# Blocks 3 to 8 of a gated MLP in pairs: first layer as seven products of half-size sums, weight sums streamed from DRAM

## The chip, the cores and the metric

The kernel runs on one core of one Trainium2 chip. The metric is the time of one execution in device microseconds (us). The kernel before took 1048.71 us, the median of 3 runs (1047.23 to 1051.59 us). The profile is that of one further execution.

## The reference

`q`, `k` and `v` hold 8 batches of 8 heads with 576 rows of 64 values. First comes an attention whose keys and values are averaged over groups of 8 rows, so that 576 queries meet 72 keys. Its output, 4608 tokens of 512 values, goes through a root-mean-square norm and a gated MLP. In short:

```python
k_p = k.reshape(B, H, 72, 8, D).mean(axis=3);  v_p = v.reshape(B, H, 72, 8, D).mean(axis=3)
attn = softmax(q @ k_p.T / 8)
x = (attn @ v_p) as 4608 tokens x 512
xn = x / sqrt(mean(x * x) + 1e-6) * rms_g
g = xn @ w_gate;  val = xn @ w_val                  # 512 x 1536 each
out = (g * sigmoid(g) * val) @ w_out                # 1536 x 512
```

All arrays are float32.

## The kernel before, in words

**Precision.** Each operand of a large product is split into a high part (a copy in the type float32r) and a low part (the remainder). A product is then three matmuls: high weight by high x, low weight by high x, high weight by low x. `xh`, `xl` are the parts of x, `hh`, `hl` those of the hidden layer; the tiles of `w1` and `w2` (printed as `w`) hold both parts of the weights and stay on chip.

**MLP.** The tokens go in 9 blocks of 512 (`NBLK`, `NB`). d_ff is cut into 12 slices f of 128 (`NF`), d_model into 4 chunks (`NC`). For each block and f, `mm1` (L490) makes the gate slice with 12 matmuls into one PSUM bank, ScalarE takes silu of it (`gate`, L497), another 12 matmuls make the value slice into the other bank, VectorE multiplies (`val`, L502), ScalarE copies the high part `hh` (L506), VectorE subtracts for the low part `hl` (L510), and `mm2` (L521) adds 12 matmuls of the f before into four banks `po`. So one f is 36 matmuls of 512 columns. `psg` alternates between banks 2 and 3, `po` has banks 4 to 7, the attention banks 0 and 1. After f = 11 the four `po` are copied out (L527) and stored (L528).

**Attention.** It goes by head pairs, four to a batch. SyncE (SP) issues all DMAs, in program order: k (L200), q (L208) and v (L219) of a head pair come in; `s_heads` (L282) makes the scores with 10 small matmuls for each of two heads; `s_soft` (L291 to L299) is the softmax on VectorE, ScalarE and GpSimd (POOL); `s_turn` (L304) transposes the probabilities into `sq`, and twelve small DMAs (L309) gather `sq` into `pt`; `s_av` (L343) multiplies by the pooled values, and `s_square`, `s_join`, `s_sums`, `s_rms` (L378 to L404) make the norm of a batch once its four pairs are done. k and q of later pairs share one buffer (`qk`), v, `sq` and the squares share two buffers of one tag (`st`), `prob` is one buffer.

**Order.** A first phase in an order written out by hand (`ORDER`) holds batches 0 and 1, the conversion of the weights and block 0. What follows is written in program order and put in order by the compiler's scheduler: blocks 1 to 8, and between their steps the attention of batches 2 to 7 (`later_steps`, handed out by `more()` so that a block's tokens are ready when it starts). Blocks 7 and 8 have no attention beside them. `split_x` (L462, L463) multiplies by the gain and splits the tokens of a block.

## Time and profile before

| | |
|---|---|
| median of 3 runs | 1048.71 us |
| the profiled execution's own time | 1049.04 us |
| its span | 1047.3 us |
| mean granted TensorE clock | 0.980 |
| DMA, mean over the span | 62 GB/s |

The span is the time from the first to the last instruction of the core; 1.7 us of the execution lie around it. PE is TensorE's matmul, PEld its weight load, DVE is VectorE, ACT is ScalarE, POOL is GpSimd, SPq is SyncE's queue that issues the DMAs. A group's row gives busy time and the mean of one in ns, then the idle time just before its instructions and what ended it. A matmul's record lasts longer than its slot, because matmuls are pipelined: the slot is the distance between starts.

### The profile page before, as it was taken

The page shows a single profiled execution, that of the slowest core. Times are in us where ns is not written, and L with a number is a line of the kernel's source. Part 1 is how long each engine was busy: PE and PEld are TensorE (multiplying, and loading weights), DVE is VectorE, ACT ScalarE, POOL GpSimd, SP SyncE. Part 2 cuts the span into 40 slices and gives each one's busy share as a digit, 9 for nine tenths or more (in the row PEclk, how much of TensorE's full clock was granted, in tenths as well). Part 3 has the DMA queues.
Part 4 walks back from the last instruction along what each step waited for, and adds up shares of the span by engine and source line. Part 5 has one row for each costly group of instructions (what it writes and reads, how often), then busy time and mean ns, then how long its engine had stood idle before and what let it go on. Part 6 is the DMA issues. An engine that isn't in the chain of part 4 may idle for free.

```text
span 1047.3 us, 13134 instructions
## 1 busy us (share of the span) xinstructions
PE 1026.6 (98%) x4994; PEld 816.2 (78%) x4994; DVE 506.3 (48%) x857; ACT 416.6 (40%) x771; POOL 115.9 (11%) x108
## 2 busy tenths in 40 slices
PE   7899998999999999999999999999999999999998
PEld 6677776777877777777877787778777888888886
DVE  6799985635455446344653455445452431122112
ACT  5767664433443345333533354335342431121111
POOL 2313430111001100111001101110011000000000
PEclk8599999999999999999999999999999999999999
DMA  9445412222022201221122103210210010001001
GB/s 292 133 163 177 170 62 72 74 76 74 25 73 73 58 25 50 77 66 36 43 75 54 57 3 108 55 53 12 88 36 14 1 41 1 1 1 41 1 1 40
DMA packets 38702, 65.44 MB, mean 62 GB/s; under 512 B 6384, under 2 KB 20208, under 8 KB 37360
## 3 DMA queue, kind: packets, MB, share of 16 engines
q1 hardware_dynamic: 38640, 64.61, 20.3%
q8 instruction: 39, 0.64, 0.3%
q14 instruction: 23, 0.19, 0.1%
HBM read 47.19 MB, written 9.44 MB: 54 GB/s over the span
## 4 chain that ended last, share of the span: by engine, by line
PE 88%; DVE 5%; DMA 2%; ACT 2%; issue 1%; SPq 0%; ACTq 0%
PE psg L490 53%; PE po L521 27%; PE pss L282 4%; PE psx L343 3%; DVE wt L140 1%; DMA wx<-w 1%; DVE wt L144 1%; DMA main<-kT 1%; DVE wt L136 1%; ACT prob L260 1%; PE psr L412 1%; DVE w L162 0%; PE pst L323 0%; PE psb L436 0%; DMA q<-qT 0%
## 5 line engine op out<-in xcount | busy, mean ns | idle before, releaser
L490 PE MATMUL psg<-xh,w 128*128 128x512 f32 x1728 | 541.3, 395 | 2.9 <-ACT xh L462 2.9
L490 PEld LDWEIGHTS psg<-xh,w 128*128 128x128 f32 x1728 | 322.3, 189 | 82.9 <-ACT xraw L350 3.4
L490 PE MATMUL psg<-xl,w 128*128 128x512 f32 x864 | 338.2, 392 | 0.0
L521 PE MATMUL po<-w,hh 128*128 128x512 f32 x864 | 223.3, 395 | 0.0
L502 DVE TENSOR_TENSOR act<-act,psg 128x512 f32<-128x512 f32 x108 | 73.6, 682 | 288.1 <-PE psg L490 254.5
L521 PEld LDWEIGHTS po<-w,hh 128*128 128x128 f32 x864 | 162.6, 188 | 37.7
L490 PEld LDWEIGHTS psg<-xl,w 128*128 128x128 f32 x864 | 162.6, 188 | 35.5 <-DVE xl L463 0.7
L506 ACT CAST hh<-act 128x512 fp32r<-128x512 f32 x108 | 67.1, 622 | 212.5 <-DVE act L502 212.4
L497 ACT ACTIVATE act<-psg 128x512 f32<-128x512 f32 x108 | 64.5, 597 | 204.8 <-PE psg L490 202.6
L521 PE MATMUL po<-w,hl 128*128 128x512 f32 x432 | 122.4, 395 | 0.4 <-DVE hl L510 0.4
L521 PEld LDWEIGHTS po<-w,hl 128*128 128x128 f32 x432 | 79.5, 188 | 20.3 <-DVE act L502 2.0
L510 DVE TENSOR_TENSOR hl<-act,hh 128x512 fp32r<-128x512 f32 x102 | 70.0, 686 | 40.9 <-ACT hh L506 38.5
L299 POOL TENSOR_TENSOR prob<-prob,sm 128x360 f32<-128x360 f32 x48 | 38.7, 826 | 446.2 <-DVE sm L297 257.9
L497 ACT ACT_TABLE_LOAD x40 | 51.3, 1283 | 47.8 <-PE psg L490 26.6
L291 DVE TENSOR_REDUCE mx<-pss 128x5 f32<-128x360 f32 x48 | 23.4, 528 | 49.8 <-PE pss L282 49.6
L304 DVE STREAM_TRANSPOSE sq<-prob 128x960 f32<-128x960 f32 x24 | 28.3, 1179 | 38.8 <-POOL prob L299 34.6
L384 POOL TENSOR_TENSOR acc<-acc,sq 128x576 f32<-128x576 f32 x21 | 30.7, 1461 | 146.4 <-ACT sq L378 146.4
L239 DVE TENSOR_REDUCE pv<-v 72x128 f32<-72x1024 f32 x28 | 34.0, 1214 | 22.8 <-PE psx L343 21.5
L282 PEld LDWEIGHTS pss<-pk,q 64*128 64x128 f32 x560 | 34.5, 193 | 12.0 <-issue 8.9
L282 PE MATMUL pss<-pk,q 64*128 64x72 f32 x560 | 38.6, 283 | 1.8 <-DVE own L329 0.9
L294 ACT ACTIVATE prob<-prob 128x360 f32<-128x360 f32 x48 | 23.1, 505 | 31.9 <-DVE prob L293 31.8
L343 PE MATMUL psx<-pt,pv 72*64 72x256 f32 (+2 forms) x224 | 35.4, 429 | 0.0
(90 smaller groups left out, 701.2 us busy)
## 6 DMA issues: line engine op xcount, KB each, us to landing
wx<-w SPq DMA_DIRECT2D x10, 1024.0 KB
v<-vN SPq DMA_DIRECT2D x32, 288.0 KB
out<-o SPq DMA_DIRECT2D x36, 256.0 KB
wx<-w SPq DMA_DIRECT2D x16, 512.0 KB
k<-kT SPq DMA_DIRECT2D x28, 288.0 KB
q<-qT SPq DMA_DIRECT2D x28, 288.0 KB
pt<-sq SPq DMA_DIRECT2D x96, 40.0 KB
pt<-sq SPq DMA_DIRECT2D x96, 32.0 KB
```

The source lines that it names most:

```text
L239: nc.vector.tensor_reduce(pv, s["v"], AX.X, ALU.add)
L282: nc.tensor.matmul(s["ps", h][:, t * SP:(t + 1) * SP], s["q"][r, o:o + P], s["pk"][r, :], start=True, stop=True)
L299: nc.gpsimd.tensor_tensor(pr, pr, sm[:, :, None].broadcast_to(shape), ALU.mult)
L304: nc.vector.transpose(sq.rearrange("p b g j -> p g b j"), prob.rearrange("p g (b j) -> p g b j", b=3))
L343: nc.tensor.matmul(ps[r, :n], s["pv"][:, r], s["pt"][:, h, tok], start=True, stop=True)
L384: nc.gpsimd.tensor_add(acc[b], acc[b], st[b, p]["sq"])
L490: nc.tensor.matmul(ps[:, :NB], w[:, c, cols], x[c], start=(j == 0), stop=(j == len(todo) - 1))
L497: nc.scalar.activation(t, ps[:, :NB], AF.Silu)
L502: nc.vector.tensor_mul(t, t, ps[:, :NB])
L506: nc.scalar.copy(a, st["act"])
L510: eng.tensor_sub(l, st["act"], hh[i, f].bitcast(F32))
L521: nc.tensor.matmul(po[i][t], x[i, f][:, t * P:(t + 1) * P], w, start=(f == 0 and k == 0), stop=(f == NF - 1 and k == 2))
```

## The change

**Blocks 1 and 2** are computed as before, with two additions. The attention is handed out faster: three batches (2 to 4) are finished here, where before it was one for each block; the other three batches are spread over the pairs (3,4) and (5,6). And `w_parts` makes, for each f, the seven weight operands of a seven-product scheme and writes them to DRAM: three are blocks of the first-layer weights and are copied by DMA (L532, eight a slice), four are sums and differences, made on POOL (L537 to L542), split by ScalarE (L546) and POOL (L547) and written (L548). The sums use the tag `st`, the split ones the tag `out`, of two buffers each.

**Blocks 3 to 8** go in pairs (3,4), (5,6), (7,8). For one f the pair's tokens (two blocks), the two halves of d_model and the two kinds of columns (gate, value) make a 2x2 by 2x2 block product. In place of eight block products of 6 matmuls, seven are made (`PRODUCTS`, in Winograd's form), so 42 matmuls in place of 48. The operands of x (`XP`: three blocks, four sums) are made once for a pair by `halves`; the weight operand of each product, 256 KB, comes from DRAM through a ring of 8 slots (`next_part`, L608), and the next load is written behind each product. The results are combined on VectorE (L828, L837, L841, L845, L851, L852, L855) and ScalarE (a copy L825, silu L834 and L842); the products alternate between bank 2 (`px`, `pv`) and bank 3 (`py`, `pz`, `pw`). The first block's `mm2` is run in two halves inside the next f; its hidden layer is split at L658 (`hh`) and L662 (`hl`, one buffer as before). The second block's hidden layer is kept in `hb`, and its twelve `mm2` run after the pair's twelve f, with `halves` of the next pair written between them.

**Smaller edits.** The norm's last step multiplies by the gain as well: four operations of 288 elements (L419) for each half in place of one of 4x288 (L404). `ones` is one column that is broadcast. `keep_tail` keeps the end of a batch that the next pair needs.

What the order shows. SyncE's queue in block 1, before: between the loads of one head pair and its gathering copies stands nothing else (`k`, `v`, `q`, `pt` as above).

```order
L219 DMA v_3_1914<-vN 72x1024
L200 DMA k_3_1912<-kT 128x576
L208 DMA q_3_1933<-qT 128x576
L309 DMA pt_2_1937<-sq_2_1935 32x2x128 x2
L309 DMA pt_2_1937<-sq_2_1935 32x2x160 x2
```

The same place in the changed kernel; `parts` are the weight operands in DRAM, `wt` the split sums.

```order
L214 DMA k_3_1898<-kT 128x576
L532 DMA parts_2349<-w_4_772 128x2x128 x4
L548 DMA parts_1807<-wt_1_1914 128x512
L233 DMA v_3_1900<-vN 72x1024
L548 DMA parts_1807<-wt_2_1918 128x512
L222 DMA q_3_1928<-qT 128x576
L532 DMA parts_2349<-w_4_772 128x2x128
L532 DMA parts_2579<-w_5_906 128x2x128
L548 DMA parts_1807<-wt_3_1922 128x512
L548 DMA parts_1807<-wt_4_2004 128x512
L532 DMA parts_2579<-w_5_906 128x2x128
L323 DMA pt_2_1932<-sq_2_1930 32x2x128 x2
```

Two of the four writes of a slice now stand ahead of the q load and two ahead of the gathering copies of the pair; each waits for POOL and ScalarE to make its tile.

TensorE in block 1 before, f = 9 with the `mm2` of f = 8 behind it (the end of the value slice, `psg_9_1`):

```order
L490 MATMUL psg_9_1_3189<-xh_2_2460,w_9_1213 128x512 x2
L490 MATMUL psg_9_1_3189<-xl_2_2464,w_9_1213 128x512
L490 MATMUL psg_9_1_3189<-xh_3_2461,w_9_1213 128x512 x2
L490 MATMUL psg_9_1_3189<-xl_3_2465,w_9_1213 128x512
L521 MATMUL po_0_2637<-w_8_1138,hl_8_3155 128x512
L521 MATMUL po_1_2638<-w_8_1138,hl_8_3155 128x512
L521 MATMUL po_2_2639<-w_8_1138,hl_8_3155 128x512
L521 MATMUL po_3_2640<-w_8_1138,hl_8_3155 128x512
L521 MATMUL po_0_2637<-w_8_1138,hh_8_3153 128x512 x2
```

TensorE in the last pair of the changed kernel: the last product of f = 2 (`pw_2`, weight operand `wp_2_6`), then f = 3 (`xp` are the operands of x).

```order
L614 MATMUL pw_2_7732<-xp_S_7347,wp_2_6_7651 128x512 x6
L614 MATMUL px_3_7763<-xp_A_7283,wp_3_0_7666 128x512 x6
L614 MATMUL py_3_7773<-xp_S_7326,wp_3_1_7682 128x512 x6
L614 MATMUL px_3_7763<-xp_A_7368,wp_3_2_7692 128x512 x3
L673 MATMUL po_0_7603<-w_2_604,hl_2_7760 128x512
L673 MATMUL po_1_7604<-w_2_604,hl_2_7760 128x512
L673 MATMUL po_0_7603<-w_2_604,hh_2_7758 128x512 x2
L673 MATMUL po_1_7604<-w_2_604,hh_2_7758 128x512 x2
L614 MATMUL px_3_7763<-xp_A_7368,wp_3_2_7692 128x512 x3
L614 MATMUL pz_3_7799<-xp_S_7389,wp_3_3_7707 128x512 x6
```

Before, 24 matmuls of L490 stand between the value slice of an f and the first `mm2` that reads its `hl`; now 15 matmuls stand between the last product of an f and that `mm2`. At the end of a pair none do (f = 11, then the second block's f = 0):

```order
L614 MATMUL pw_11_8514<-xp_S_7347,wp_11_6_8445 128x512 x6
L673 MATMUL po_0_7603<-w_11_1418,hl_11_8538 128x512
L673 MATMUL po_0_7603<-w_11_1418,hh_11_8536 128x512 x2
L673 MATMUL po_1_7604<-w_11_1418,hl_11_8538 128x512
L673 MATMUL po_1_7604<-w_11_1418,hh_11_8536 128x512 x2
L673 MATMUL po_2_7605<-w_11_1418,hl_11_8538 128x512
```

There the `mm2` of f = 11 follows the last product directly.

VectorE at the end of pair (3,4), between the combination of f = 11 and its `hl`: `acc` and `xraw` belong to the norm of batch 6, `xp_A` to `halves` of the next pair.

```order
L419 SCALAR_TENSOR_TENSOR xraw_4844<-xraw_4844,gcol,acc_4854 128x288 x4
L837 TENSOR_TENSOR u_4227<-u_4227,pz_11_5636 128x512
L416 RECIPROCAL acc_4854<-acc_4854 128x288
L841 TENSOR_TENSOR hb_8_5242<-u_4227,pv_11_5646 128x512
L419 SCALAR_TENSOR_TENSOR xraw_4844<-xraw_4844,gcol,acc_4854 128x288
L845 TENSOR_TENSOR u_4227<-u_4227,pw_11_5657 128x512
L419 SCALAR_TENSOR_TENSOR xraw_4844<-xraw_4844,gcol,acc_4854 128x288 x3
L855 TENSOR_TENSOR hb_8_5242<-hb_8_5242,u_4227 128x512
L851 TENSOR_TENSOR u_4227<-u_4227,pw_11_5657 128x512
L577 TENSOR_TENSOR xp_A_5826<-u_4227,xp_A_5826 128x2x320
L852 TENSOR_TENSOR act_11_5634<-act_11_5634,u_4227 128x512
```

The norm of a batch now stands among the combining operations; before, `L404` stood beside `L502` and `L510` alone.

The diff, cut to its core:

```diff
+FIRST = 3
+PRODUCTS = (("A11", "B11"), ("S2", "T2"), ("A12", "B21"), ("S3", "T3"), ("A22", "T4"), ("S1", "T1"), ("S4", "B22"))
+RING = [f"x{j}{c}" for c in range(NC) for j in "hl"]
...
-        x = xraw[b][:, :, tok]
-        nc.vector.tensor_mul(x, x, r[:, None, :].broadcast_to([P, NC, n]))
+        for c in range(NC):
+            x = xraw[b][:, c, tok]
+            nc.vector.scalar_tensor_tensor(x, x, gcol[:, c:c + 1], r, ALU.mult, ALU.mult)
...
+    def w_parts(f, k):
...
+        if k is None:
+            for name in PARTS:
+                if name in BLOCKS:
+                    for h in (0, 1):
+                        nc.sync.dma_start(wparts[f][PARTS.index(name)][:, h], block(W1[f][:, h].bitcast(F32), name))
+            return
+        G = nc.gpsimd
+        if k == 0:
+            t = sb2.tile([P, NC, 2 * P], F32, tag="st", name=f"wsum{f}")
+            G.tensor_add(t, W1[f][:, 0].bitcast(F32), W1[f][:, 1].bitcast(F32))
+            d = WP["sum"] = sb2.tile([P, 4, 2, P], F32, tag="st", name=f"wdif{f}")
+            G.tensor_sub(d[:, 0], block(t, "B12"), block(t, "B11"))
...
+        d = WP["sum"][:, k - 1]
+        y = sb2.tile([P, 2, 2, P], F32R, tag="out", name=f"wt{f}_{k}")
+        nc.scalar.copy(y[:, 0], d)
+        G.tensor_sub(y[:, 1], d, y[:, 0].bitcast(F32))
+        nc.sync.dma_start(wparts[f][PARTS.index(f"T{k}")], y.bitcast(F32))
...
+    def halves(i, n):
...
+        nc.scalar.copy(X[:, 0], y)
+        V.tensor_sub(X[:, 1], y, X[:, 0].bitcast(F32))
...
+    def next_part():
+        n = len(ring)
+        if n < len(todo_parts):
+            i, f, k = todo_parts[n]
+            w = ring[i, f, k] = sb1.tile([P, 2, 2, P], F32R, tag=RING[n % len(RING)], name=f"wp{i}_{f}_{k}")
+            nc.sync.dma_start(w.bitcast(F32), wparts[f][k])
+
+    def product(i, f, k, ps, start, stop):
+        w, x = ring[i, f, k], XP[i, PRODUCTS[k][0]]
+        todo = [(c, h) for c in range(2) for h in ((0, 0), (1, 0), (0, 1))]
+        for j, (c, (a, b)) in enumerate(todo):
+            nc.tensor.matmul(ps[:, :NB], w[:, a, c, :], x[:, b, c, :],
+                             start=start and j == 0, stop=stop and j == len(todo) - 1, skip_group_check=not start)
+        next_part()
...
-    mm2(*pend)
+    for i in range(FIRST, NBLK, 2):
+        j = i + 1
...
+            x = bank(2, f"px{i}_{f}")
+            product(i, f, 0, x, True, True)
+            nc.scalar.copy(h, x)
+            y = bank(3, f"py{i}_{f}")
+            product(i, f, 1, y, True, True)
+            nc.vector.tensor_add(u2, h, y)
+            more()
+            if pend:
+                mm2(*pend, (0, 1))
+            product(i, f, 2, x, False, True)
+            t = st["act"] = sb1.tile([P, NB], F32, tag="act", name=f"act{i}_{f}")
+            nc.scalar.activation(t, x, AF.Silu)
+            y = bank(3, f"pz{i}_{f}")
+            product(i, f, 3, y, True, True)
+            nc.vector.tensor_add(u3, u2, y)
+            more()
+            x = bank(2, f"pv{i}_{f}")
+            product(i, f, 4, x, True, True)
+            nc.vector.tensor_sub(h, u3, x)
+            nc.scalar.activation(h, h, AF.Silu)
+            y = bank(3, f"pw{i}_{f}")
+            product(i, f, 5, y, True, True)
+            nc.vector.tensor_add(u3, u3, y)
+            more()
+            if pend:
+                mm2(*pend, (2, 3))
+            pend = (i, f)
+            product(i, f, 6, y, False, True)
+            nc.vector.tensor_add(u2, u2, y)
+            nc.vector.tensor_mul(t, t, u2)
+            act_hi(i, f)
+            act_lo(i, f, nc.vector)
+            nc.vector.tensor_mul(h, h, u3)
+            more()
+        mm2(*pend)
+        pend = None
+        for f in range(NF):
+            st["act"] = hb[f // 4][:, f % 4]
+            act_hi(j, f)
+            act_lo(j, f, nc.vector)
+            mm2(j, f)
+            if j + 1 < NBLK and f < len(XPARTS):
+                halves(j + 1, ORDER_X[f])
```

## The prediction

> **What bounds the kernel now.** I read the page first, for the busy shares and the chain.

> ```profile
> span 1047.3 us, 13134 instructions
> ...
> PE 1026.6 (98%) x4994; PEld 816.2 (78%) x4994; DVE 506.3 (48%) x857; ACT 416.6 (40%) x771; POOL 115.9 (11%) x108
> ...
> PE 88%; DVE 5%; DMA 2%; ACT 2%; issue 1%; SPq 0%; ACTq 0%
> PE psg L490 53%; PE po L521 27%; PE pss L282 4%; PE psx L343 3%; DVE wt L140 1%; DMA wx<-w 1%; DVE wt L144 1%; DMA main<-kT 1%; DVE wt L136 1%; ACT prob L260 1%; PE psr L412 1%; DVE w L162 0%; PE pst L323 0%; PE psb L436 0%; DMA q<-qT 0%
> ```

> TensorE is the bound: the two layers of the MLP (L490, L521) are 80% of the span in the chain that ends last. So a matmul that goes is worth a whole slot. What a slot is shows the chain in order of time, in blocks 7 and 8, where no attention runs.

> ```profile
> 843.00 5.47 PE psg L490 x24
> ...
> 1024.32 5.47 PE psg L490 x24
> ```

> From 843.00 to 1024.32 lie 22 slices f, each 24 matmuls of L490 and 12 of L521: 181.32 / 22 = 8.242 us a slice, 8.242 / 36 = 0.2289 us a matmul, without a wait. A block with attention beside it, from the table of windows (block 3):

> ```profile
> 401.60:512.40 110.80, 110.80 (x550) 87.77 (x549) 52.97 (x96) 44.93 (x69) 10.78 (x11) 1.00 0.19 54
> ```

> 110.80 less 12 x 8.242 = 98.9 leaves 11.9 us, or 2.98 us of TensorE for each of four head pairs. TensorE does not stop there either. So before has hardly a wait after the first phase, and whatever the change makes TensorE wait is added in full.

> **What is removed.** In each pair of blocks and each f, 42 matmuls replace 48: 3 x 12 x 6 = 216 slots of 0.2289 = 49.4 us less. Moved attention (four head pairs of 2.98 us into blocks 1 and 2) sums to nothing on TensorE.

> **What is added, one: the chain of a pair's f.** The operations of the hidden layer and the hand-over from TensorE:

> ```profile
> L502 DVE TENSOR_TENSOR act<-act,psg 128x512 f32<-128x512 f32 x108 | 73.6, 682 | 288.1 <-PE psg L490 254.5 <-issue 33.6
> L510 DVE TENSOR_TENSOR hl<-act,hh 128x512 fp32r<-128x512 f32 x102 | 70.0, 686 | 40.9 <-ACT hh L506 38.5 <-PE po L521 2.4
> L506 ACT CAST hh<-act 128x512 fp32r<-128x512 f32 x108 | 67.1, 622 | 212.5 <-DVE act L502 212.4
> L497 ACT ACT_TABLE_LOAD x40 | 51.3, 1283 | 47.8 <-PE psg L490 26.6 <-DVE hl L510 21.0
> ...
> 334.23 0.39 PE L490 MATMUL psg<-xl,w 128*128 128x512 f32 x1
> 334.72 0.69 DVE L502 TENSOR_TENSOR act<-act,psg 128x512 f32<-128x512 f32 x1 [6.50 <-PE psg L490]
> 335.44 0.62 ACT L506 CAST hh<-act 128x512 fp32r<-128x512 f32 x1 [2.90 <-DVE act L502]
> ```

> The last matmul's slot ends at 334.23 + 0.23 = 334.46 and VectorE starts at 334.72, 0.26 later; ScalarE follows VectorE after 0.03. In the pair, `hl` of an f comes after the last product through u2, act, `hh` and `hl`: 0.26 + 0.69 + 0.69 + 0.03 + 0.62 + 0.05 + 0.69 = 3.0 us, and its `mm2` stands 15 slots behind, 15 x 0.2289 = 3.4 us. The cover is 0.4 us, where before 24 slots (5.5 us) less 2.3 left 3.2. The banks have as little: a bank is refilled 6 slots (1.37 us) after its product, and one VectorE operation takes 0.26 + 0.69 = 0.95 of it, 0.4 to spare; a table load of 1.28 us ahead of silu does not fit. The VectorE work is eight operations of 0.69 in 12.4 us, so it is place in the queue, not load, that can stall. Where the next f's u2 (L828, which waits 12 slots, 2.75) is ahead of `hl` in VectorE's order, `hl` is there after 2.75 + 0.26 + 0.69 + 0.69 = 4.4, about 1 us late. I take 0.17 us for each of 36 f, 6 us; 0 if all covers hold, 10 if `hl` is late by 0.3 each time.

> **Two: attention inside the pairs.** Eleven to twelve head pairs run there, each with these on VectorE, the first three twice:

> ```profile
> L293 DVE TENSOR_TENSOR prob<-pss,mx 128x360 f32<-128x360 f32 x48 | 23.7, 522 | 0.0
> L291 DVE TENSOR_REDUCE mx<-pss 128x5 f32<-128x360 f32 x48 | 23.4, 528 | 49.8 <-PE pss L282 49.6
> L296 DVE TENSOR_REDUCE sm<-prob 128x5 f32<-128x360 f32 x48 | 23.0, 521 | 0.3
> L304 DVE STREAM_TRANSPOSE sq<-prob 128x960 f32<-128x960 f32 x24 | 28.3, 1179 | 38.8 <-POOL prob L299 34.6 <-DMA pt<-sq 4.2
> L228 DVE TENSOR_REDUCE pk<-k 128x72 f32<-128x576 f32 x28 | 21.0, 751 | 22.9 <-DMA k<-kT 22.9
> L239 DVE TENSOR_REDUCE pv<-v 72x128 f32<-72x1024 f32 x28 | 34.0, 1214 | 22.8 <-PE psx L343 21.5 <-DMA v<-vN 1.1
> L402 DVE RECIPROCAL acc<-acc 128x288 f32<-128x288 f32 x12 | 23.4, 1952 | 13.1 <-ACT acc L401 13.0
> L463 DVE SCALAR_TENSOR_TENSOR xl<-xraw,gcol,xh 128x320 fp32r<-128x320 f32 x8 | 4.3, 543 | 2.3 <-ACT xh L462 2.3
> ```

> 2 x (0.522 + 0.528 + 0.521) + 1.179 + 0.751 + 1.214 = 6.3 us a head pair. VectorE takes them in order among the combining operations, whose banks have 0.4 us to spare: each of the three long ones that comes at a wrong time costs up to 0.8. Before, a bank had 12 slots, so they cost nothing. I take 0.85 us for 11 head pairs, 9.5, and 2.5 for the norms of three batches: 12, between 5 (one collision in two head pairs) and 25 (three in each).

> **Three: the seams.** After the last product of a pair nothing is left for TensorE but the `mm2` that waits for `hl`: the chain of 3.0 and a weight load of about 0.2, 3.2 us, at three seams. `hl` has one buffer, so the second block's first `hl` waits until the `mm2` of f = 11 has read it, 1 us more: 4.2 each, 12.6. At the end of pair (3,4) the norm of batch 6 stands in VectorE's queue ahead of `hl`: two reciprocals of 1.95 and eight scaled copies of some 0.5 (the 0.543 of 128x320 bounds one) are 8 us, of which I take 6.4 as uncovered. At both inner seams `halves` puts seven steps into the second block's f.

> ```profile
> L162 DVE TENSOR_TENSOR w<-wt,w 128x1024 fp32r<-128x1024 f32 x6 | 7.3, 1215 | 0.0
> ```

> Four sums at 2 x 1.215 and three splits at 1.215 are 13.4 us, with twelve `hl` 21.7, against 12 x 12 slots of TensorE, 33 us: hidden but for the start, 1.8. Together 12.6 + 6.4 + 1.8 = 20.8, taken as 21, between 14 and 28.

> **Four: the clock at the seams.** The one long wait of before outside the first phase shows what follows one (timeline and windows):

> ```profile
> 178.61 0.73 PE L490 MATMUL psg<-xh,w 128*128 128x512 f32 x2 [2.91 <-ACT xh L462]
> 186.52 1.34 PE L282 MATMUL pss<-pk,q 64*128 64x72 f32 x20 [0.18 <-DMA q<-qT]
> ...
> 178.00:181.00 3.00, 2.39 (x7) 1.55 (x8) 2.69 (x8) 2.96 (x8) 0.00 (x0) 0.85 0.97 295
> 181.00:184.00 3.00, 3.00 (x9) 2.34 (x9) 1.90 (x4) 0.48 (x1) 0.00 (x0) 0.58 0.76 205
> ```

> After 2.91 us without work the granted clock fell to 0.58, and 24 matmuls took 186.34 - 178.61 = 7.73 in place of 5.47, 2.3 us more. All three seams wait 3.2 or more, but the last has little left behind it: 2 x 2.3, taken as 4, between 0 and 7. [...]

> **Five: the first pair's start.** Its ring loads and the last of its operands come behind gathering copies and a dense VectorE queue: 4, between 0 and 8 (one burst of copies, below).

> **Six: blocks 1 and 2.** SyncE issues in order. A burst of gathering copies and what follows it:

> ```profile
> 195.54 8.21 SPq L309 DMA_DIRECT2D pt<-sq  x12
> 203.85 0.38 SPq L200 DMA_DIRECT2D k<-kT  x1
> 205.12 1.18 DVE L304 STREAM_TRANSPOSE sq<-prob 128x960 f32<-128x960 f32 x1 [4.15 <-DMA pt<-sq]
> ...
> L162 POOL TENSOR_TENSOR w<-wt,w 128x1024 fp32r<-128x1024 f32 x4 | 10.0, 2503 | 21.4 <-ACT w L158 21.4
> L299 POOL TENSOR_TENSOR prob<-prob,sm 128x360 f32<-128x360 f32 x48 | 38.7, 826 | 446.2 <-DVE sm L297 257.9 <-DVE sm L298 188.3
> ```

> The burst issues for 8.2 us and lands 205.12 - 203.75 = 1.4 later. `wdif` shares the two buffers of `sq`, so POOL begins it only then. POOL takes 2.5 us for 1024 elements; one of 256 lies between 2.5 / 4 = 0.63 and the 0.83 of 360, and I take 0.75. Four differences are 3.0, two low parts 1.5, their writes' landing 1.4 (the `out` tag has two buffers), the other two low parts 1.5, their writes' issue 0.8; then the next burst. A round is 17.8 us. Three batches and one head pair ahead are 13 rounds, 231, and with the first softmax (186.52 to 195.54, 9.0) and a last step of about 10, 250. TensorE has 24 x 8.242 + 12 x 2.98 = 233.6. The difference is 17 (a prolonged wait at `psx` for `pt`, since TensorE too is in order); 2 if rounds overlap, 40 if the four writes are each late by a landing.

> **The sum.** 6 + 12 + 21 + 4 + 4 + 17 = 64 us of waits against 49.4: 1049.0 + 14.6 = 1063.6, so 1064. The profiled execution is 0.3 above the median of the runs, which is within the spread; the span lies 1.7 below it.

> **The rivals.**

> *The queues stay ahead* (faster). Every wait above supposes that an operation stands where I put it in its queue. If a round in blocks 1 and 2 takes under 233.6 / 13 = 18.0 us with its ends overlapped, TensorE sets the pace there and term six falls to 1. VectorE at some 6.3 us more in each second f is likewise far from full, so that collisions come to 8 and the chain to 2; the seams' floor is 12.6 and the norm is covered: 14; clock 3, start 1. Waits 29, 1049.0 - 49.4 + 29 = 1029. For it: VectorE is busy 48%, ScalarE 40%. Against: 0.4 us of cover.

> *No change.* Half of term six and a cheaper seam, waits of 44 to 55: 1049 (1044 to 1054). For it stands that each term's lower half suffices.

> *The ring starves* (slower still). A ring load is issued when its slot is read, some 7 products (9.6 us) to a whole f (12.4) ahead of its use. Behind a burst of 8.2 and a landing of 1.4, with up to four loads queued, it comes up to 4 us late, at each of 11 bursts: 44 more, 1108. The loads before:

> ```profile
> k<-kT SPq DMA_DIRECT2D x28, 288.0 KB
> ```

> A pair needs 7 x 256 KB in 12.36 us, 148 GB/s; in the window 178 to 181 above, loads of 288 KB moved at 295 GB/s. So bandwidth speaks against it and SyncE's order for it. [...]

> **How the numbers follow.** The forecast as reasoned (its own range 1054 to 1090) 0.44, the queues ahead 0.31, no change 0.13, the starving ring 0.12. A difference of 0.5% (5 us) is about what a measurement of this kernel can tell. So faster 0.31, same 0.13, slower 0.56. The range: all low ends together, 0 + 5 + 14 + 0 + 0 + 2 = 21 us of waits, give 1021, so it begins at 1020; at the top, terms six and two halfway to their high ends (+18) and the ring late at a third of the bursts (+14) give 1096.

> **What would show it.** In the changed profile: periods of 54 slots in pair (7,8), 12.4 us if clean, 12.7 with term one; idle time ahead of `po` reading `hl` at each seam, 3 us and more; idle ahead of `psx` in blocks 1 and 2 released by `pt`; granted clock under 1.0 after the seams. Idle time ahead of a product released by a DMA of `wp` means the ring. The forecast is wrong if blocks 1 and 2 show no such idle time, or if TensorE's idle time after block 0 sums to under 45 us.

## The result, and the profile after

The changed kernel took 1115.49 us, the median of 4 runs (1110.75 to 1116.32), against 1049.18 us for the kernel before on the same chip: a ratio of 1.062, with a 95% interval of 1.058 to 1.066. It is slower by 66 us, and not by the 15 that were forecast; the time lies above the range. The matmuls went as counted (49.4 us), so TensorE lost some 116 us to other things where 64 were expected. The page of the changed kernel:

```profile
span 1113.0 us, 14084 instructions
...
PE 1038.7 (93%) x4778; PEld 790.1 (71%) x4778; DVE 669.7 (60%) x1090; ACT 451.8 (41%) x843; POOL 221.6 (20%) x216
...
PEclk8599998999989789999999999999999999999999
...
PE 60%; DVE 16%; DMA 7%; issue 5%; SPq 4%; ACT 4%; POOL 3%; POOLq 0%; DVEq 0%; ACTq 0%
```

TensorE now has 60% of the chain that ends last, where it had 88%, and the row of the granted clock is under 9 tenths in the slices 12, 14 and 15 of the 40, which lie in blocks 1 and 2. TensorE's busy time did not fall although 216 matmuls went (1038.7 us, 1026.6 before): where the granted clock was 0.50 each took longer. In one such stretch, from 446.71 to 449.70, seven matmuls of 512 columns start 0.43 us apart, against 0.23 at a clock of 1.00. The table of windows shows the stages: first blocks 1 and 2 of the kernel before, then of the changed kernel blocks 1 and 2 and the three pairs. A stage runs from its first matmul to the first of the next; the columns are those of the first line.

```profile
core 0: us, PE busy (x) PEld busy (x) DVE busy (x) ACT busy (x) POOL busy (x), PEclk, DMA share, GB/s
178.61:401.60 222.99, 222.81 (x1107) 176.04 (x1108) 114.63 (x208) 92.34 (x144) 22.76 (x24) 0.99 0.22 61
```

```profile
181.11:491.56 310.45, 275.59 (x1296) 200.63 (x1297) 192.84 (x334) 145.54 (x247) 143.09 (x148) 0.91 0.48 142
491.56:717.86 226.30, 216.66 (x996) 162.96 (x995) 146.74 (x253) 91.14 (x137) 18.49 (x19) 0.99 0.50 151
717.86:919.00 201.14, 195.68 (x862) 151.85 (x861) 106.21 (x167) 64.64 (x98) 7.40 (x7) 1.00 0.43 127
919.00:1109.09 190.09, 186.41 (x787) 147.17 (x785) 76.74 (x113) 37.22 (x63) 0.00 (x0) 0.99 0.39 115
```

How many head pairs lie in blocks 1 and 2 is read from the scores (20 records each) and from psx (8 each):

```profile
L296 PE MATMUL pss<-pk,q 64*128 64x72 f32 x320 | 25.2, 277 | 8.9 <-DMA q<-qT 7.8 <-ACT xraw L364 0.7 <-DVE xraw L366 0.4
L357 PE MATMUL psx<-pt,pv 72*64 72x256 f32 (+1 forms) x112 | 21.6, 467 | 12.7 <-DMA pt<-sq 9.2 <-issue 3.3
```

That is 16 scores and 14 psx, on the mean 15 head pairs. The counts of matmuls in the windows also show that the last 12 of block 2's `mm2` run in pair (3,4), and that six matmuls of the next pair's first product run ahead of the border of (5,6) and of (7,8). The stages against their slots:

| stage | time | slots | lost |
|---|---|---|---|
| blocks 1 and 2 | 310.5 | 24 x 8.242 + 15 x 2.98 - 12 x 0.2289 = 239.8 | 71 |
| pair (3,4) | 226.3 | 12 x 66 x 0.2289 + 6.5 x 2.98 + 18 x 0.2289 = 204.8 | 22 |
| pair (5,6) | 201.1 | 181.3 + 2.5 x 2.98 = 188.8 | 12 |
| pair (7,8) | 190.1 | 181.3 - 6 x 0.2289 = 179.9 | 10 |

The three pairs lost 44 us together. Blocks 1 and 2, which keep the old form, lost 71. (Block 1 began 2.5 us later than before; in the traces of all runs it begins between 176.7 and 181.6.) The waits of TensorE that the profile names in the whole changed kernel, the largest first:

```profile
PE po L673 <- DVE hl L662: 13.8, 12, 3.2
PE psx L357 <- DMA pt<-sq: 9.2, 6, 3.9
PE pss L296 <- DMA q<-qT: 7.8, 8, 1.5
...
PE px L614 <- DMA wp<-parts: 0.9, 1, 0.9
```

Before, the hand-over from hl cost 0.4 us in all, the q loads 0.2, and psx had no wait:

```profile
PE po L521 <- DVE hl L510: 0.4, 1, 0.4
...
PE pss L282 <- DMA q<-qT: 0.2, 1, 0.2
```

The ring hardly ever made TensorE wait (0.9 us).

**The clock in blocks 1 and 2.** One less the granted clock, summed over blocks 1 and 2, makes 27 us there and 1.7 in the same blocks before. TensorE was at work for 47.4 of the 54.6 us at half clock (16 windows at 0.50), so by the clock's share 23.7 us of work were lost to it. TensorE was idle for 34.9 us (310.45 less 275.59). How the rest of the 71 parts was not measured. In the changed kernel's trace every change of the clock falls on a grid of 3.413 us with one phase for the whole run: 27 stretches at one clock in a row last 1 to 114 whole steps of it. Two pairs of neighbouring grid windows:

```profile
214.61:218.02 3.41, 1.95 (x24) 1.50 (x22) 2.16 (x2) 0.81 (x2) 2.39 (x3) 1.00 0.89 283
218.02:221.44 3.42, 3.42 (x12) 2.63 (x10) 1.85 (x4) 0.32 (x1) 1.37 (x1) 0.50 0.38 110
```

```profile
276.05:279.46 3.41, 1.72 (x9) 1.25 (x8) 2.38 (x2) 1.53 (x4) 1.42 (x2) 1.00 0.18 45
279.46:282.87 3.41, 3.41 (x30) 2.69 (x29) 3.41 (x3) 2.42 (x4) 3.25 (x5) 1.00 0.68 197
```

In the first window TensorE did 20 small matmuls of the scores and 4 of 512 columns, was idle 1.46 us, and the next window ran at half clock. In the second pair's first window it was idle longer, 1.69 us, but did 7 of 512 columns, and the clock held. Some 15 of 512 columns fit in a window (3.413 / 0.2289).

### The profile page after: what moved, and what is told of

It is laid out like the page before. It is cut to its first block, busy times and chain, and to the rows that moved or that the text cites. A ratio compares the mean times of both kernels' runs of the same rounds, so it can differ in the third digit from the quotient of the medians.

```text
span 1113.0 us, 14084 instructions
## 1 busy us (share of the span) xinstructions
PE 1038.7 (93%) x4778; PEld 790.1 (71%) x4778; DVE 669.7 (60%) x1090; ACT 451.8 (41%) x843; POOL 221.6 (20%) x216
## 4 chain that ended last, share of the span: by engine, by line
PE 60%; DVE 16%; DMA 7%; issue 5%; SPq 4%; ACT 4%; POOL 3%; POOLq 0%; DVEq 0%; ACTq 0%
PE po L673 20%; PE pw L614 8%; PE px L614 7%; PE psg L642 6%; PE pz L614 4%; PE pv L614 4%; PE py L614 4%; SPq L323 4%; PE pss L296 3%; PE psx L357 2%; DVE xraw L419 1%; DMA q<-qT 1%; DVE wt L154 1%; DMA k<-kT 1%; DVE acc L416 1%
## 5 line engine op out<-in xcount | busy, mean ns | idle before, releaser
L642 PE MATMUL psg<-xh,w 128*128 128x512 f32 x576 | 196.2, 421 | 3.0 <-ACT xh L507 2.9
L673 PEld LDWEIGHTS po<-w,hh 128*128 128x128 f32 x864 | 166.4, 193 | 38.8 <-issue 0.8
L642 PEld LDWEIGHTS psg<-xh,w 128*128 128x128 f32 x576 | 113.6, 201 | 37.6 <-issue 7.9
L642 PE MATMUL psg<-xl,w 128*128 128x512 f32 x288 | 119.9, 419 | 0.0
L614 PE MATMUL px<-xp_A,wp 128*128 128x512 f32 x432 | 118.5, 397 | 0.9 <-DMA wp<-parts 0.9
L614 PE MATMUL pw<-xp_S,wp 128*128 128x512 f32 x432 | 113.5, 397 | 2.0 <-DVE u L845 1.5
L614 PEld LDWEIGHTS pw<-xp_S,wp 128*128 128x128 f32 x432 | 80.4, 188 | 24.1 <-DVE u L845 3.7
L614 PEld LDWEIGHTS px<-xp_A,wp 128*128 128x128 f32 x432 | 80.5, 188 | 22.2 <-DMA wp<-parts 1.8
L837 DVE TENSOR_TENSOR u<-u,pz 128x512 f32<-128x512 f32 x36 | 24.7, 686 | 86.3 <-PE pz L614 86.2
L642 PEld LDWEIGHTS psg<-xl,w 128*128 128x128 f32 x288 | 57.5, 200 | 16.8 <-issue 3.5
L662 DVE TENSOR_TENSOR hl<-act,hh 128x512 fp32r<-128x512 f32 x66 | 49.1, 743 | 32.5 <-ACT hh L658 32.5
L825 ACT COPY hb<-px 128x512 f32<-128x512 f32 x36 | 21.1, 585 | 111.7 <-PE px L614 111.7
L658 ACT CAST hh<-act 128x512 fp32r<-128x512 f32 x72 | 44.7, 620 | 52.0 <-DVE act L852 29.5
L614 PE MATMUL pz<-xp_S,wp 128*128 128x512 f32 x216 | 57.0, 397 | 0.7 <-DVE u L828 0.7
L614 PE MATMUL pv<-xp_A,wp 128*128 128x512 f32 x216 | 56.8, 398 | 0.0
L842 ACT ACTIVATE hb<-hb 128x512 f32<-128x512 f32 x36 | 22.7, 632 | 83.4 <-DVE hb L841 83.1
## 6 DMA issues: line engine op xcount, KB each, us to landing
v<-vN SPq DMA_DIRECT2D x32, 288.0 KB
k<-kT SPq DMA_DIRECT2D x28, 288.0 KB
```

The costliest lines, as they stand in the source:

```text
L614: nc.tensor.matmul(ps[:, :NB], w[:, a, c, :], x[:, b, c, :], start=start and j == 0, stop=stop and j == len(todo) - 1, skip_group_check=no ...
L642: nc.tensor.matmul(ps[:, :NB], w[:, c, cols], x[c], start=(j == 0), stop=(j == len(todo) - 1))
L658: nc.scalar.copy(a, st["act"])
L662: eng.tensor_sub(l, st["act"], hh[i, f].bitcast(F32))
L673: nc.tensor.matmul(po[i][t], x[i, f][:, t * P:(t + 1) * P], w, start=(f == 0 and k == 0), stop=(f == NF - 1 and k == 2))
L837: nc.vector.tensor_add(u3, u2, y)
```

## The experiments

Each time is the median of two or four runs, beside runs of the kernel before on the same chip (1049 to 1051 us).

| run | us | ratio, 95% interval |
|---|---|---|
| changed kernel | 1115.5 | 1.062 (1.058 to 1.066) |
| e1 operands of one slice | 1077.5 | 1.027 (1.024 to 1.030) |
| e2 copies only | 1075.9 | 1.025 (1.022 to 1.028) |
| e3 sums only | 1118.5 | 1.066 (1.063 to 1.069) |
| e4 writes on ScalarE's queue | 1125.8 | 1.073 (1.068 to 1.078) |
| e5 no first sum | 1091.6 | 1.039 (1.035 to 1.043) |
| e6 no writes | 1112.3 | 1.058 (1.055 to 1.061) |
| e7 split bursts | 1108.7 | 1.055 (1.044 to 1.066) |
| e8 even pace | 1117.9 | 1.064 (1.061 to 1.067) |
| e9 one tile | 1104.0 | 1.052 (1.049 to 1.056) |
| e10 one tile, split bursts | 1117.6 | 1.065 (1.060 to 1.070) |
| e11 one tile, pairs from block 5 | 1093.4 | 1.041 (1.038 to 1.044) |
| e12 one slice, split bursts | 1094.6 | 1.043 (1.039 to 1.047) |
| e13 filler | 1120.2 | 1.068 (1.064 to 1.071) |
| e14 one tile, VectorE | 1096.5 | 1.046 (1.042 to 1.050) |
| e15 as e14, pairs from block 5 | 1077.7 | 1.027 (1.023 to 1.031) |
| e16 two hl | 1108.6 | 1.057 (1.054 to 1.060) |
| e17 one slice, pairs from block 5 | 1066.6 | 1.016 (1.014 to 1.018) |

### What in blocks 1 and 2: the making of the operands, or the pace

e1 makes the operands of one slice, and the ring reads that slice for all twelve; the matmuls stay the same in number, though they no longer compute this MLP:

```diff
-    todo_w = [(f, k) for f in range(NF) for k in (None, 0, 1, 2, 3, 4)]
+    todo_w = [(0, k) for k in (None, 0, 1, 2, 3, 4)]
...
-            nc.sync.dma_start(w.bitcast(F32), wparts[f][k])
+            nc.sync.dma_start(w.bitcast(F32), wparts[0][k])
```

> The weight operands are made for one slice f alone and every ring load reads that slice; eleven twelfths of the copies, sums, splits and writes are left out of blocks 1 and 2, and the attention keeps its faster pace. Blocks 1 and 2 took 313 us in the changed kernel (178.6 to 491.7), where 24 slices and some 13 head pairs are worth 236 us of TensorE. Theory A (making the operands is what holds the attention up): these blocks fall to 240 to 255 us and the time to 1040 to 1058 us. Theory B (the faster pace of the attention holds TensorE up by itself): the blocks stay at 290 or more, the time at 1090 or more.

```profile
177.40:448.97 271.57, 255.99 (x1297) 192.43 (x1297) 176.47 (x335) 132.41 (x206) 47.84 (x49) 0.96 0.30 86
```

Neither: 38 us went, and blocks 1 and 2 still took 271.6 us, 32 more than their 239.8 of slots. So the making of the operands costs 38, and about 32 are lost with hardly any of it: 15.6 of idle TensorE (271.57 less 255.99), 10 by the clock, and some 6 that no run parts. What else the change puts in these blocks is the faster attention; that it is the cause of the 32 is argued, not shown. For it speaks where the idle time stands: some 12 of the 15.6 us ahead of the attention's own matmuls.

```profile
L296 PE MATMUL pss<-pk,q 64*128 64x72 f32 x320 | 23.6, 279 | 4.8 <-DMA q<-qT 4.7
L357 PE MATMUL psx<-pt,pv 72*64 72x256 f32 (+1 forms) x112 | 18.3, 425 | 5.5 <-DMA pt<-sq 4.7 <-PE psx L357 0.7
L413 PE MATMUL psr<-sums,ones 128*128 128x288 f32 x12 | 2.8, 303 | 1.8 <-DVE sums L405 1.8
```

e2 and e3 part the making into copies and sums; the ring reads slice 0 for what is not made:

```diff
-    todo_w = [(f, k) for f in range(NF) for k in (None, 0, 1, 2, 3, 4)]
 e2:
+    todo_w = [(f, k) for f in range(NF) for k in (None, 0, 1, 2, 3, 4) if f == 0 or k is None]
 e3:
+    todo_w = [(f, k) for f in range(NF) for k in (None, 0, 1, 2, 3, 4) if f == 0 or k is not None]
```

> All copies of weight blocks to DRAM (eight a slice) are made, the sums for one slice alone. Theory A1 (POOL, the shared buffers of sq, v, wsum and wdif, and the writes that wait for them make the round long): within 12 us of the run with one slice. Theory A2 (SyncE's issue time of 96 small copies makes the round long): at least half of the loss is still there, 1080 us or more.

> All sums, splits and their writes are made, the copies of blocks for one slice alone. Theory A1: 1095 us or more, nearly the changed kernel's 1115. Theory A2: 1075 us or less.

The copies cost nothing that can be measured (1075.9 against 1077.5); the sums cost all of it (1118.5). There are 72 copies, six for a slice: three blocks in two halves each, and not eight as the text on the change has it. SyncE's time to issue them is not the price.

### What in the sums: the writes, the buffers or POOL's time

e4 moves copies and writes to ScalarE's queue (`nc.scalar.dma_start`), e6 leaves the writes of all slices but one out (`if f == 0:` ahead of L548); its ring reads slice 0 for the sums.

> All copies and writes of weight operands are issued from ScalarE's queue in place of SyncE's. If their place in SyncE's order ahead of the q load and the gathering copies is what counts, 1050 to 1085 us. If the shared buffers and POOL's order count, 1100 us or more; ScalarE then also waits at the writes, ahead of its exponentials, and it can be slower than 1115.

> All sums and splits are made, but only the first slice's are written to DRAM, so that 44 writes that wait in SyncE's queue for POOL are left out; the ring reads the first slice's sums. Theory W: 1085 us or less. Theory S: 1100 us or more. Between them, both.

Without the writes it is 3 us less (1112.3), which the two intervals don't tell from nothing, and moving copies and writes makes it 10 slower. The prediction had 2.2 us for the writes' landing and issue in every round; next to none of that is on the path.

e5 takes the differences from the high parts alone; e9 makes the same sums in the same order of rounding, but in one tile:

```diff
 e5:
-            t = sb2.tile([P, NC, 2 * P], F32, tag="st", name=f"wsum{f}")
-            G.tensor_add(t, W1[f][:, 0].bitcast(F32), W1[f][:, 1].bitcast(F32))
+            t = W1[f][:, 0].bitcast(F32)
 e9:
-            d = WP["sum"] = sb2.tile([P, 4, 2, P], F32, tag="st", name=f"wdif{f}")
-            G.tensor_sub(d[:, 0], block(t, "B12"), block(t, "B11"))
...
+            b11, b12, b21, b22 = WP["sum"] = [block(t, x) for x in ("B11", "B12", "B21", "B22")]
+            G.tensor_sub(b11, b12, b11)
+            G.tensor_sub(b12, b22, b12)
+            G.tensor_sub(b22, b22, b11)
+            G.tensor_sub(b21, b22, b21)
```

> The differences are taken from the high parts of the weights alone: the sum of 1024 elements on POOL and its tile wsum are left out, so that of the two buffers that sq, v and the squares share only one is taken by a slice. The sums cost 38 us (1115 against 1077 with one slice). Theory S (the shared buffers couple POOL's work to the bursts and the v loads): 1088 to 1102 us. Theory P (POOL's time itself): 12 x 2.5 us of POOL less and no more than a tenth of it on the path, 1108 to 1114. Theory W (the writes that wait in SyncE's queue): unchanged, 1113 to 1118.

> The same four sums with the same operations on POOL, but each difference is written over a block of wsum that is no longer needed, so that wdif is gone and a slice takes one of the two shared buffers in place of two. Theory S (the shared buffers): 1088 to 1100 us, as without the first sum (1091.6). Theory P (POOL's 2.5 us for the first sum was what that run saved): 1108 to 1117.

e5 saves 24 us and e9, which frees the buffer but keeps the sum, 11.5. If such savings add up, which no run tests, about 11.5 of the 38 are the shared buffer, 12.4 the first sum's time on POOL, at most 3 the writes, and the rest the differences and splits. Much of what is saved is clock. Blocks 1 and 2 of e9:

```profile
181.28:481.53 300.25, 269.17 (x1317) 194.92 (x1317) 196.09 (x345) 147.47 (x252) 145.20 (x150) 0.95 0.49 146
```

TensorE is idle 31.1 us where it was 34.9, but the loss to the clock is 15 where it was 27. How the buffer acts is seen in the chain of the changed kernel, in order of time:

```profile
390.89 1.17 POOL wdif L539
...
393.50 0.74 POOL wdif L542
394.25 3.55 DMA v<-vN
397.83 1.23 DVE pv L253
...
399.14 1.19 DVE sq L318
...
402.00 0.64 SPq L323
```

The v load is issued when POOL has done with the buffer of `wsum` (394.25), VectorE waits for v, and behind that wait in VectorE's order stands the transposition that the next burst of gathering copies needs: 11 us from POOL's first difference to the burst.

e14 gives the sums in one tile, and the low parts of the split ones, to VectorE (`G = nc.vector`).

> The sums in one tile, and made by VectorE in place of POOL (VectorE takes 1.2 us for 1024 elements where POOL takes 2.5). Theory P (POOL's time in the round, 12 us of the 38): 1085 to 1098. Rival (VectorE is 60% busy in blocks 1 and 2 and its queue gets the wait in POOL's place): 1104 or more.

1096.5 us: 7.5 us below e9. The runs of the two kernels do not overlap (at most 1100.5 here, at least 1101.8 there), though their intervals do a little. So POOL's speed was part of the round, though VectorE is the busier engine (60% against POOL's 20% in the changed kernel). In the changed kernel POOL took 2.49 us for the first sum, of 128x1024, and VectorE 1.22 for an operation of that size (L598); a difference, of 128x256, took POOL 0.82 and an operation of that size VectorE 0.42 (L591, L594):

```profile
L537 POOL TENSOR_TENSOR wsum<-w 128x1024 f32<-128x1024 f32 x12 | 29.8, 2486 | 5.6 <-DMA pt<-sq 3.3 <-DMA v<-vN 1.6
L539 POOL TENSOR_TENSOR wdif<-wsum 128x256 f32<-128x256 f32 x12 | 9.8, 817 | 28.2 <-DMA pt<-sq 21.0 <-DVE pv L253 5.8 <-issue 1.3
```

### The rounds: bursts, pace, and where the pairs begin

e7, e10 and e12 issue every second gathering copy from ScalarE's queue:

```diff
-                nc.sync.dma_start(
+                (nc.scalar if a % 2 else nc.sync).dma_start(
                     t[32 * i:32 * i + n, :, o:o + w],
```

> Six of the twelve gathering copies of each head pair are issued from ScalarE's queue, so that a burst takes about 4 us of SyncE's queue in place of 8. Theory B (the burst is the longest link of a round, and rounds pace blocks 1 and 2): up to 4 us less in each of 14 rounds, 1065 to 1095 us. Rival (ScalarE pays 3.6 us a burst ahead of its own work, and the round is held elsewhere): 1110 to 1130.

> One tile for the sums and six of the twelve gathering copies on ScalarE's queue. If buffers and bursts are two separate holds: about 7 us below the run with one tile alone. If the same rounds are meant: no difference, or some us more by ScalarE's issue time.

> Weight operands for one slice alone, and half of each burst on ScalarE's queue. 30 us were lost in blocks 1 and 2 without the sums. If SyncE's burst of 8 us is the long link of those rounds: 1058 to 1070 us. If not: 1073 to 1085, with ScalarE's issue time.

7 us less on the changed kernel (with an interval that takes in the changed kernel's own ratio), 14 more beside one tile, 17 more beside one slice. The waits of ScalarE in e7 show the price: its queue waits at a copy whose `sq` isn't there and then issues six copies, up to 8.2 us, and `hh` stands behind them.

```profile
ACT hh L658 <- DMA pt<-sq: 38.9, 6, 8.2
```

So whether the burst's 8 us are the long link can't be told from these runs; the other queue costs as much as it frees.

e8 delays batch 5 to block 3:

```diff
+    goals.append((single + 15, goals[-1][1]))
     for i in range(FIRST, NBLK - 2, 2):
-        goals.append((goals[-1][0] + (15 if i == FIRST else 0) + 4 * NF, ends[min(B, -(-(i + 4) * NB // S)) - 3]))
+        goals.append((goals[-1][0] + 4 * NF, ends[min(B, -(-(i + 4) * NB // S)) - 3]))
```

> Batch 5 starts with block 3 and not in the last part of block 2, so that two head pairs fewer run in blocks 1 and 2. Theory B (each round there costs TensorE some 5 us beyond its own work): blocks 1 and 2 come down by 15 to 18 us, of which 6 is moved work, and the time is 1100 to 1108. Rival (the last blocks' batches have to be ready anyway and the lost time moves to pair (3,4)): 1112 to 1119.

```profile
180.93:479.98 299.05, 269.21 (x1221) 198.36 (x1221) 178.94 (x303) 135.00 (x232) 140.31 (x143) 0.90 0.47 140
479.98:721.40 241.42, 226.51 (x1071) 169.77 (x1070) 157.30 (x283) 100.92 (x151) 23.55 (x24) 0.97 0.50 151
```

The rival holds: blocks 1 and 2 come down by 11 us, of which 2.5 head pairs of moved work are 7.5, pair (3,4) goes up by 15, and the time is the same within the noise (1117.9). A head pair moved from one crowded place to the next brings nothing.

e11, e15 and e17 begin the pairs at block 5 (`FIRST = 5`, and one buffer for the pooled k and the softmax's small tiles): with one tile on POOL, with one tile on VectorE, with the operands of one slice.

> One tile for the sums, and the pairs begin at block 5: blocks 1 to 4 as before, the sums spread over four blocks, five batches of attention in four blocks in place of three in two, 144 matmuls (33.0 us) less than before in place of 216; the pooled k and the small tiles of the softmax have one buffer, to make room. If waits come from crowding two blocks: blocks 1 to 4 lose 25 us or less, the two pairs 9 and 25: 1049 - 33 + 59 = 1075 or less. If each slice and each round costs the same wherever it is: 1085 to 1100.

> The sums in one tile on VectorE, and the pairs beginning at block 5. If the two help separately: 1093 less 6 to 18 us, 1075 to 1087. If not: 1090 or more.

> Weight operands for one slice alone (the rest left out), pairs beginning at block 5: what the pairs would be worth if their weight operands cost nothing and the attention had four blocks in place of two. 33.0 us of slots less than before; the two pairs lost 24 us beyond their slots in the runs from block 5. If the attention's pace in four blocks (some 22 head pairs, where before had 16) loses 10 us or less: 1042 to 1052. If each head pair over the old pace costs some 4 to 5 us, as in blocks 1 and 2 without sums: 1060 to 1075.

e11 fell into the second alternative, 11 us under e9; e15 gained separately, to 1077.7, the fastest here with all operands made. e17 takes the sums away from it and is still 1.6% slower than before:

```profile
177.42:664.81 487.39, 474.95 (x2364) 364.58 (x2363) 271.25 (x518) 213.51 (x335) 64.26 (x68) 0.98 0.25 72
```

48 slices and 22 head pairs, less the 12 matmuls that run in the next pair, are 395.6 + 65.6 - 2.7 = 458.5; 29 are lost with hardly any operand made, 12.4 of it idle and 8.5 by the clock. No start of the pairs that was run pays: at block 5 33.0 us of slots are saved, the two pairs lose about 25 beyond their slots, and the blocks ahead of them 29.

### The clock

e13 adds four matmuls of 512 columns ahead of the first psx of a head pair; the scheduler puts them some slots earlier:

```diff
+        if 2 <= b <= 5 and u == 0:
+            for _ in range(4):
+                nc.tensor.matmul(ps, W2[0][:, 0, :P], W2[0][:, 0, :], start=True, stop=True)
```

> Four matmuls of 512 columns whose result is overwritten stand in TensorE's order ahead of the first psx of each head pair of batches 2 to 5, 13 us of extra slots for 14 head pairs in blocks 1 and 2. There the clock fell to half in whole stretches of 3.41 us, after stretches with at most 4 matmuls of 512 columns; 27.3 us were lost to it. Theory C (a sparse stretch brings the half clock, and a wait before psx takes extra work at no cost): the loss to the clock falls to 15 us or less, TensorE's idle time by some 10, and the time is 1100 to 1115. Rival (the extra work only adds its slots, the waits move along): 1123 to 1135, with a loss to the clock as before.

Half and half. The loss to the clock fell from 27 to 15 us while 60 matmuls (13.7 us) were added, as theory C has it; but the waits moved along, as the rival has it:

```profile
177.46:492.37 314.91, 281.05 (x1368) 206.62 (x1367) 196.92 (x342) 144.68 (x248) 141.27 (x150) 0.95 0.47 139
```

TensorE is idle for 33.9 us (34.9 before the filler). So most of the work was paid for by the clock and not by the waits: the blocks took some 5 us more, and 1120 us in all is no gain.

### The seams

e16 gives hl two buffers (`sb2.tile` for `sb1.tile` in `act_lo`); to make room, the pooled k and the softmax's small tiles have one.

> hl has two buffers (the pooled k and small tiles of the softmax have one, to make room). By the prediction's third term one buffer costs 1 us at each of the three seams: 1109 to 1114 us, and the first mm2 of a second block no longer waits for hl. Rival (the chain through hh and hl sets it, not the buffer): 1114 to 1118.

1108.6: the time asked for, but not at the place. From the start of the last product to the end of TensorE's work it is 42.5 us (43.2 in the changed kernel), 0.7 less for one seam, and the first wait there stays 2.88:

```profile
1064.31 0.79 PE L673 MATMUL po<-w,hl 128*128 128x512 f32 x1 [2.88 <-DVE hl L662]
```

Blocks 1 and 2, which have the second buffer too, took 5.4 us less (305.1). So at a seam the chain sets the wait, and the buffer little.

## Why the prediction was wrong

**What is removed** was right: slots of 0.2289 us, 216 of them.

**The chain of a pair's f** was under-sized. Pair (7,8), chain in order of time:

```profile
944.29 1.48 PE po L673 x6
...
1058.27 1.48 PE po L673 x6
```

Nine periods in 113.98 us make 12.66 a slice: 0.30 beyond 12.36, where 0.17 was taken; 36 slices make 11 us and not 6. Only 0.1 of it is hl coming late. Six matmuls of a product take 1.40 us from start to start and not 1.373, seven times 0.027 a slice; why they do was not tested. The prediction looked for waits and took every slot for equal.

**The seams** had the chain right and the rest of the term too large. The last one, from the timeline:

```profile
1065.87 1.56 PE L614 MATMUL pw<-xp_S,wp 128*128 128x512 f32 x6
...
1068.91 0.62 ACT L658 CAST hh<-act 128x512 fp32r<-128x512 f32 x1 [4.28 <-DVE act L852]
...
1069.56 0.69 DVE L662 TENSOR_TENSOR hl<-act,hh 128x512 fp32r<-128x512 f32 x1 [0.68 <-ACT hh L658]
1070.31 0.50 PE L673 MATMUL po<-w,hl 128*128 128x512 f32 x1 [2.88 <-DVE hl L662]
...
1078.45 1.20 PE L673 MATMUL po<-w,hl 128*128 128x512 f32 x4 [0.38 <-DVE hl L662]
```

2.88 us of idle where 3.2 were worked out (of these 0.2 for a weight load; those of L521 took 0.19 on the mean before), and 0.38 for the one buffer where 1 was. The norm ahead of `hl` at pair (3,4)'s end cost little, though 6.4 was taken for it: TensorE was idle for 3.24 us there. The first waits at the two inner seams:

```profile
677.30 0.51 PE L673 MATMUL po<-w,hl 128*128 128x512 f32 x1 [3.24 <-DVE hl L662]
...
881.36 0.50 PE L673 MATMUL po<-w,hl 128*128 128x512 f32 x1 [1.48 <-DVE hl L662]
```

At the middle seam six matmuls of the next pair's first product fill the time ahead. All waits for `hl` at the three seams sum to 9 us, where the third term had 21. Behind the last wait 24 matmuls (5.5 us) take from 1070.31 to 1078.45, 8.1: a clock window of 3.41 us at 0.50, from 1071.35, takes 1.7 of it. After block 2 one clock window fell at pair (3,4)'s end and one here, 3.4 us in all where the fourth term had 4. The three pairs lost 44 us; terms one to five were 6 + 12 + 21 + 4 + 4 = 47. That these agree is in part luck: the first term was too small by 5 and the third too large. How attention, start and seam share the 22 of pair (3,4) was not parted by a run.

**Blocks 1 and 2** is the step that failed: 17 us, between 2 and 40, where 71 were lost. Two figures of its sum were too small, and one loss was missing. The number of rounds: "Three batches and one head pair ahead are 13 rounds", but the pace's next goal begins 15 places before block 2 ends, and 15 bursts start there. And the round, 17.8 us:

```profile
198.15 8.22 SPq L323 DMA_DIRECT2D pt<-sq  x12
...
488.77 8.10 SPq L323 DMA_DIRECT2D pt<-sq  x12
```

14 rounds in 290.6 us are 20.8. In the prediction's own sum they give 290.6 + 9 + 10 = 310 against 242.5 of slots, 67 lost. This shows how far off the term's sizes were, but it proves no cause: 20.8 is the measured time over the number of rounds, and whatever made TensorE wait is in it, the clock too. In the kernel with one slice 15 bursts start from 195.59 to 436.74, 17.2 us each. With the sums all but gone a round is thus nearly as long as was predicted with them; the sums add 3.6. What makes the round long was named only in part: the wait of wdif for sq is there, the writes are hardly (3 us or less, e6), and the way through the v load and VectorE's order was missed. The wait that was foreseen, psx for pt, is 9.2 of TensorE's 34.9 us of idle time in these blocks; 7.8 stand ahead of the scores, for q, and 8.4 ahead of psr, for the norm's sums.

**The clock** was charged at two seams and nowhere else. In blocks 1 and 2 it took 23.7 of the 71. The prediction quoted one wait of 2.91 us and the half clock after it, and read from it that long waits bring it. The grid windows tell more: a wait of 1.46 us did so too (214.61:218.02, above), and one of 1.36 us with 1.23 of it in this window, where small matmuls of the attention filled much of the rest:

```profile
289.70:293.12 3.42, 2.19 (x11) 1.06 (x12) 3.42 (x8) 2.81 (x7) 3.26 (x6) 1.00 0.51 180
293.12:296.53 3.41, 3.41 (x10) 2.67 (x9) 0.98 (x5) 0.65 (x2) 2.84 (x4) 0.50 0.65 184
```

**The rivals.** The ring did not starve: 0.9 us of TensorE waiting for `wp`, with 252 loads of 256 KB. (The 295 GB/s that the prediction read for loads alone are of a window that follows two stores of `out`, issued at 177.3 and 177.8, and so may hold those too.) *The queues stay ahead* and *no change* fell with term six. What stays open is what makes 29 to 32 us of loss with the sums gone. The faster attention is argued for it, and no run kept the pairs at the old pace of the attention. Idle time there is spread over psx, pss, psr and the blocks' ends in pieces of at most 6.3 us, and about a third is the clock.

## What to carry to other kernels

Before trusting a saving of matmuls, list what has to be made ready for it and by when, count the rounds of that work from the order of instructions itself, not from the plan's words, and multiply by the length of one round against TensorE's work in it: here 15 bursts, 20.8 us apart, stood against 242 us of TensorE, 16 for each. In these traces a short wait beside small matmuls cost a second time by the clock, and one beside large matmuls mostly did not: after windows with at most 4 matmuls of 512 columns the clock was at 0.50 in 33 of 39 cases, after windows with 7 or more in 1 of 458. A buffer tag shared by a load, a transposition and POOL's sums tied three queues together here (11 us from POOL's first difference to the burst); computing in place in one tile took 11 us off without any other change.

## What the runs showed of the hardware

In pair (7,8) of the changed kernel a product of 6 matmuls into a bank of its own took 1.40 us from start to start (starts at 946.31, 947.71, 949.11 and 950.51), 0.027 more than six slots of the old first layer (6 x 0.2289).
